# Spreading weight conversions over a loop, and moving preparation work by one step, in a clustered-attention and two-layer expert kernel

## The chip, the cores and the metric

The kernel runs on one core of a Trainium2 chip. A core has a matrix engine (TensorE, PE in the profile, with its weight loads as PEld), a vector engine (VectorE, DVE), an activation engine (ScalarE, ACT), a general engine (GpSimd, POOL) and a queue engine (SyncE, SP) that only starts transfers. Each engine takes its own instructions in the order in which the program gives them; engines wait for each other by semaphores. Transfers started by SP and by POOL are carried out by 16 DMA engines. The metric is the device time of one execution in microseconds; lower is better.

## What is computed

Three stages, one after the other, in float32:

```python
# 1. attention inside clusters: 2 batches x 8 heads, 768 positions, 64 wide, 16 centroids per head
q_assign = argmax(normalize(q) . normalize(centroids))     # k_assign likewise
scores = where(q_assign == k_assign, q @ k.T / 8, -1e9)
attn = softmax(scores) @ v                                 # -> x, 1536 tokens x 512
# 2. first layer: w_in 512 x 2048, w_out 2048 x 512
h = x @ w_in;  x = maximum(0.01 * h, h) @ w_out
# 3. mixture of 8 experts, top 1, with a skip test per token
skip = x @ w_skip;  e = argmax(x @ w_gate);  gate = softmax(x @ w_gate).max()
out = x + (skip > 0) * gate * (relu(x @ w1[e]) @ w2[e])
```

## The kernel before, in words

**Precision.** Most products are made in pieces. An operand is split into a rounded part (`hi`, in names `whii`, `whio`, `gh`, `xh`, `UA`) and the rest (`lo`, in names `wloi`, `wloo`, `gl`, `xl`), and three products are added: hi x hi, hi x lo, lo x hi. Splits are a copy on ACT (hi) and a subtraction on POOL or DVE (lo).

**Attention.** Eight pairs of heads (`p` = 0 to 7), each with 12 steps (`r` = 0 to 11, `s` = 12 p + r over all). A step takes 128 queries of one head against 768 keys. On PE it makes the scores (`st_scores`, L359: four matmuls from `UA`/`UB`, whose rows 64 to 79 hold the cluster mask, and from `VA`/`VB`, which hold the low parts), then the transposes of the probabilities of step s-3 (`st_transpose`, L414), and in every second step (r even) two pieces of attention x value for an earlier half pair (`st_av`, L433). DVE finds the row maximum, ACT makes the exponential (`st_exp`) and empties the transposes from PSUM (`st_evac`, tag T, two banks). For each half pair (`g`) the reciprocals of the row sums are transposed in `recip_rows` (L399; it too takes a bank of tag T), copied by ACT, written to a scratch in DRAM by SP, and read back spread over the partitions by POOL (`recip_load`), for `av_split` on POOL.

**Preparation of the next pairs** runs inside the steps of the pairs before. A table (`plan`, L311; `PREP`, `PREPS`) gives for each operation the step and one of four slots in a step (a0 and pa before the transposes, d and pb at the step's end). The operations are: transposes of raw q and k (`raw_pe`, PE, in bank M) and their copy (`raw_act`, ACT), the split (`raw_split`, POOL, followed by transfers on SP that rearrange halves, then `exchange`), cluster scores (`assign_pe`, `assign_act`), the argmax (`argmax_pe` on PE, `argmax_0` to `argmax_3` on DVE and POOL), the mask (`mask_pe`, `mask_dve`, `mask_dma`). `plan(d)` shifts all but the splits and exchanges by d steps. The tiles of tag M have one bank: who writes it next waits until the one before is read.

**Start.** Pair 0 is prepared ahead of the steps: its halves are exchanged by nine transfers inside the core (L490 to L504), six on SP and three on POOL, its cluster argmax runs on DVE, and `mask_first` (L272) writes the masks of queries (DVE) and keys (ACT) straight into `UA` and `UB`. Pair 1's raw copies and splits follow in the same stretch. An activation of one element (L505) loads the table of the exponential.

**Weights of the first layer.** `w_in` and `w_out` come as float64 words. 32 pieces (each 128 x 512) are loaded into staging buffers (`load_piece`, L534) and converted by five operations each (`convert_op`, L549): one on ACT (`cvu`, L557), four on DVE (L559, L561, L564, L570). Pieces 0 to 19 are converted during attention. The last twelve are converted in the first layer's loop by `conv_next(n)` (L671): it converts pairs of pieces until n of the twelve are done, and after each pair lets `load_next` put further loads on SP. Staging has two buffers for odd pieces (and, for the first, one even piece) and two for even ones; a load waits on SP until its buffer's last reader is done.

**First layer.** 48 iterations (3 blocks of 512 tokens x 16 chunks of the hidden width). Iteration i on PE: `m1_up(i)` (12 matmuls), then `m1_down(i-2)` (12 matmuls). On the others: `m1_act(i)` (`lk` on ACT, `g` on DVE, `gh` on ACT, `gl` on DVE), then the splits of the weights of i+2 (`split_i`, `split_o`: `whii` and `whio` on ACT, `wloi` and `wloo` on POOL), then `conv_next` by the line below. Chunk i=8 first reads pieces 1 to 4 of the twelve (split in iteration 6), i=12 the others (from iteration 10 on).

```python
conv_next(i + 3 if i % 2 else 0)      # before: i=1 converts four pieces, i=3, 5, 7, 9 two each
```

Of the kernel before, what the change touches and what calls it, by code (L numbers as in the profile page):

```python
# [15 lines left out]
ALU = mybir.AluOpType  # L16
AX = mybir.AxisListType
BIG = float(2.0 ** 60)
# [7 lines left out]
def kernel(  # L26
# [14 lines left out]
    nc = tc.nc  # L41
    B, H, S, D = q.shape
    NC_ = centroids.shape[1]
# [44 lines left out]
    HS = S // 2  # L88
# [82 lines left out]
    def raw_pe(p, i):  # L171
# [7 lines left out]
            nc.tensor.transpose(ps[:, j, :], src[:, 3 * half + j].rearrange("p h d -> p (h d)"), ident)  # L179
        ps_prep["raw", i] = ps  # L180

    def raw_act(p, i):
        qk, half = divmod(i, 2)
        ps = ps_prep.pop(("raw", i)).rearrange("p j c -> p (j c)")
        sc = SCALE if qk == 0 else 1.0
        nc.scalar.activation(out=raw_t[p][:, i, :], in_=ps, func=AF.Copy, scale=sc)
        if p == 1:
            raw_split(p, i)
            if half:
                exchange(p, qk)  # L190

    def first_hi(i):
        qk, half = divmod(i, 2)
# [6 lines left out]
    def raw_split(p, i):  # L200
        raw = raw_t[p]
        UA, UB, VA, VB = uv_t[p]
        qk, half = divmod(i, 2)
        cs = slice(half * HS, (half + 1) * HS)
        hi = UA[:, qk, cs]
        lo = (VA if qk == 0 else VB)[:, qk, cs]
        nc.gpsimd.tensor_scalar(out=hi, in0=raw[:, i, :], scalar1=1.0, scalar2=1.0, op0=ALU.mult, op1=ALU.mult)
        nc.gpsimd.tensor_tensor(out=lo, in0=raw[:, i, :], in1=_f(hi), op=ALU.subtract)
        if half == 1:
            dma = nc.sync.dma_start  # L210
            U, W, X, Y = (_f(t[:, qk, :]) for t in (UA, UB, VA, VB))
            dma(W[0:64], U[64:128])
            if qk == 0:
                dma(Y[0:64], X[64:128])
                dma(Y[64:128], U[64:128])
            else:
                dma(X[64:128], Y[0:64])
                dma(X[0:64], U[0:64])

    def exchange(p, qk):  # L220
        U, W, X, Y = (_f(t[:, qk, :]) for t in uv_t[p])
        if qk == 0:
            nc.sync.dma_start(X[64:128], U[0:64])
        else:
            nc.sync.dma_start(Y[0:64], W[0:64])
# [46 lines left out]
    def mask_first(h):  # L272
        U = uv_t[0][h]
        for qk in (1, 0):
            ps = (ps_m if h else ps_t)([P, S], "mps", BF16) if qk or not h else ps_a([P, S], "mps", BF16)
            for i in range(2):
                for j in range(3):
                    o = (3 * i + j) * P
                    nc.tensor.transpose(ps[64:64 + NC_, o:o + P], oh_t[0][:, j, 4 * qk + 2 * i + h, :], identb)
            ps = ps[64:64 + NC_, :]  # L280
            if qk:
                nc.scalar.activation(out=U[64:64 + NC_, 1, :], in_=ps, func=AF.Copy)
            else:
                nc.vector.tensor_scalar(out=U[64:64 + NC_, 0, :], in0=ps, scalar1=BIG, scalar2=-BIG,
                                        op0=ALU.mult, op1=ALU.add)

    def mask_pe(p):
        ps = ps_m([P, 3, P], "ohps", BF16)
# [22 lines left out]
    def plan(d):  # L311
        return [
            (d - 8, "pb", raw_pe, 0), (d - 7, "a0", raw_act, 0), (d - 7, "pb", raw_pe, 1),
            (d - 6, "a0", raw_act, 1), (d - 6, "pb", raw_pe, 2), (d - 5, "a0", raw_act, 2), (d - 5, "pb", raw_pe, 3),
            (d - 4, "a0", raw_act, 3), (d - 4, "pb", assign_pe, None),
            (d - 3, "a0", assign_act, None), (d - 3, "pb", argmax_pe, None),
            (d - 2, "d", argmax_0, None), (d - 2, "d", argmax_1, None), (d - 1, "d", argmax_2, None),
            (d, "d", argmax_3, None), (d + 1, "pb", mask_pe, None), (d + 2, "d", mask_dve, None),
            (0, "a0", raw_split, 0), (1, "a0", raw_split, 1), (2, "a0", raw_split, 2), (3, "a0", raw_split, 3),
            (3, "d", exchange, 0), (5, "d", exchange, 1), (max(d + 2, 5), "d", mask_dma, None),  # L320
        ]

    PREP = plan(0)
    PREP0 = [(3, "a0", assign_act, None), (3, "pb", argmax_pe, None), (4, "d", argmax_0, None), (4, "d", argmax_1, None),
             (5, "d", argmax_2, None), (6, "d", argmax_3, None)]
    PREP1 = [(1, "pb", assign_pe, None), (2, "a0", assign_act, None), (2, "pb", argmax_pe, None), (3, "pb", argmax_0, None), (4, "pb", argmax_1, None), (5, "d", argmax_2, None), (6, "pb", argmax_3, None), (7, "pb", mask_pe, None), (8, "d", mask_dve, None),
             (8, "d", mask_dma, None)]
    PREPS = {0: PREP0, 1: PREP1, 2: plan(4), 3: plan(2)}

    def prep(p, r, slot):  # L330
        if p >= NP:
            return
        for rr, sl, f, arg in PREPS.get(p, PREP):
            if rr == r and sl == slot:
                if arg is not None:
                    f(p, arg)
                else:
                    f(p)
                if f is raw_act and arg == 3 and 1 < p < NP - 1:
                    load_qk(p + 1)  # L340
# [141 lines left out]
    def first_lo(qk, halves=(0, 1)):  # L482
        for half in halves:
            cs = slice(half * HS, (half + 1) * HS)
            nc.vector.tensor_tensor(out=lo_k[:, half, :] if qk else VA[:, 0, cs], in0=raw_t[0][:, 2 * qk + half, :],
                                    in1=_f(UA[:, qk, cs]), op=ALU.subtract)

    Uq, Wq, Xq, Yq = (_f(t[:, 0, :]) for t in (UA, UB, VA, VB))
    Uk, Wk, Xk, Yk = (_f(t[:, 1, :]) for t in (UA, UB, VA, VB))
    nc.sync.dma_start(Wq[0:64], Uq[64:128])  # L490
    nc.sync.dma_start(Yq[64:128], Uq[64:128])
    first_lo(0, (0,))
    prep_cblk()
    first_lo(0, (1,))
    nc.sync.dma_start(Yq[0:64], Xq[64:128])
    nc.gpsimd.dma_start(Wk[0:64], Uk[64:128])
    nc.gpsimd.dma_start(Xk[0:64], Uk[0:64])
    nc.gpsimd.dma_start(Yk[0:64], Uk[64:128])
    assign_pe(0)
    first_lo(1)  # L500
    lo_kf = _f(lo_k.rearrange("p a b -> p (a b)"))
    nc.sync.dma_start(Xk[64:128], lo_kf[0:64])
    nc.sync.dma_start(Yk[64:128], lo_kf[64:128])
    nc.sync.dma_start(Xq[64:128], Uq[0:64])  # L504
    nc.scalar.activation(out=warm, in_=warm, func=AF.Exp)  # L505
    for r in range(3, 7):
        for slot in ("a0", "pa", "d", "pb"):
            prep(0, r, slot)
    load_v(0)
    for i in range(4):  # L510
# [2 lines left out]
    load_qk(2)  # L513
    mask_first(0)
    mask_first(1)

    chunks = {}
    ring_b = [None]
# [152 lines left out]
    def conv_next(n):  # L671
        while nxt[1] < min(n, len(pieces)):
            two = pieces[nxt[1]:nxt[1] + 2]
            for i_ in range(5):
                for pc in two:
                    convert_op(*pc, i_)
            nxt[1] += 2
            load_next(nxt[1] + (2 if wsp[0] is None else 4))

    for s in range(NSTEP + 12 + LAG):  # L680
        p, r = divmod(s, 12)
        if s < NSTEP:
            st_scores(s)
        conv_step(s, 0)
        preps(p, r, "a0")
        preps(p, r, "pa")
        if 0 <= s - LAG < NSTEP:
            st_transpose(s - LAG)
            st_evac(s - LAG)
        gf, rf = divmod(s, 6)  # L690
        if 0 < gf <= NSTEP // 6:
            if rf == 2:
                recip_rows(gf - 1)
            elif rf == 3:
                nc.sync.dma_start(rscr[gf - 1], rrow_t.pop(gf - 1))
        g, kt = divmod(s - 6 - LAG, 6)
        if 0 <= g < NSTEP // 6 and kt % 2:
            st_av(g, kt - 1)
            st_av(g, kt)
        if s < NSTEP:  # L700
            st_exp(s)
        if 0 <= g < NSTEP // 6 and kt == NT - 1:
            av_evac(g)
            av_split(g)
        if 0 <= g < NSTEP // 6 and kt == 3:
            recip_load(g)
        if 0 < gf <= NSTEP // 6 and rf < 2:
            recip(gf - 1, rf)
        preps(p, r, "d")
        preps(p, r, "pb")  # L710
        if r == 10 and p + 1 < NP:
            load_v(p + 1)
        conv_step(s, 1)
        if s == NSTEP:
            att_a.release()
            rt = pool("rt", "left")
            ring_b[0] = pool("ring_b", "left")
            wip[0] = pool("wi", "left")
            for c in range(NDIR // 4, NPC // 4):
                load_f32(c)  # L720
            load_next(2)
        if s == NSTEP + 4:
            for i in range(3):
                split_i(i)
# [301 lines left out]
    for i in range(NI):  # L1026
        if i == 14:
            r_consts()
        if i >= 2:
            m1_up(i)  # L1030
        for f, arg in sorted(r_tasks.get(i, ()), key=lambda x: x[1]):
            f(arg)
        step_gen(i, 0)
        if i >= 2:
            m1_down(i - 2)
        m1_act(i)
        step_gen(i, 1)
        if i + 2 < NI:
            if i:
                split_i(i + 2)  # L1040
            split_o(i + 2)
            g_, j_ = divmod(i + 2 - 2 * NFC, 4)
            if g_ >= 0 and j_ == 3:
                load_chunk(8 + 2 * g_)
                load_chunk(9 + 2 * g_)
        conv_next(i + 3 if i % 2 else 0)

    lb = NBLK - 1
    LT = lb * TPB
# [370 lines left out]
```

## Time and profile before

| | us |
|---|---|
| median of 3 runs (lowest to highest) | 690.68 (690.42 to 690.96) |
| the profiled execution | 689.63 |
| its span, first to last instruction | 687.9 |
| TensorE busy | 636.7 (93%) |
| ScalarE busy | 423.8 (62%) |
| VectorE busy | 407.4 (59%) |
| GpSimd busy | 278.2 (40%) |

Mean granted TensorE clock over the span: 0.985 of full speed. Attention's first scores start at 18.2 us, its last transposes end near 260, the first layer's loop runs from about 267 to about 555, the experts from there to the end. Times inside the span count from its start. Busy time of an engine is the sum of its instructions; PE's matmuls overlap and their ends are modelled. In a timeline a row shows start, duration, engine, line, operation, what it writes and reads, how often (rows of one kind that follow each other are merged), and in brackets the idle time of the engine before it and what ended that.

### The profile page before, as it was taken

What the parts mean: (1) busy time and instruction counts of PE and PEld (TensorE: products, weight loads), DVE (VectorE), ACT (ScalarE), POOL (GpSimd) and SP (SyncE); (2) the same over time, 40 slices, a digit from 0 to 9 for tenths busy, and PEclk for the clock granted to TensorE, in tenths of its full rate; (3) what the DMA queues carried; (4) which work ended last, traced back from release to release, by engine and by line L of the source; (5) the groups of instructions that cost most, each with busy time, mean ns of one, the idle gap of its engine ahead of it and who ended that gap; (6) DMA issues with size and microseconds to landing.
All of it is one profiled execution on the core that took longest, in us unless ns stands there. A gap on an engine that the chain in (4) does not pass through costs nothing. (4 is left out here: it accounts for less than half of the span.)

```text
span 687.9 us, 10140 instructions
## 1 busy us (share of the span) xinstructions
PE 636.7 (93%) x3587; PEld 491.8 (71%) x3587; DVE 407.4 (59%) x687; ACT 423.8 (62%) x824; POOL 278.2 (40%) x295
## 2 busy tenths in 40 slices
PE   5898999999999999499999999999999979989994
PEld 3676766666766666378888888788787868767873
DVE  5755858686776653767523213623226348999991
ACT  5887888897888885254445444445444436757870
POOL 4233636264553324363554444444444273002321
PEclk9999999999999999889999999999999999999997
DMA  8763764767656354221003000006303349989950
GB/s 196 184 189 95 196 163 140 187 172 193 167 153 171 111 183 144 104 111 61 1 3 122 1 1 0 1 0 245 122 3 122 123 163 362 339 280 333 357 192 25
DMA packets 62659, 98.31 MB, mean 143 GB/s; under 512 B 27593, under 2 KB 31659, under 8 KB 62224
## 3 DMA queue, kind: packets, MB, share of 16 engines
q1 hardware_dynamic: 59040, 88.13, 41.5%
q0 software_dynamic: 3568, 9.52, 4.2%
q8 instruction: 29, 0.48, 0.3%
q14 instruction: 22, 0.18, 0.1%
HBM read 72.47 MB, written 11.65 MB: 122 GB/s over the span
## 5 line engine op out<-in xcount | busy, mean ns | idle before, releaser
L369 DVE TENSOR_REDUCE st<-sps 128x1 f32<-128x768 f32 x96 | 91.5, 954 | 66.7 <-PE sps L366 66.3
L430 ACT ACTIVATE pt<-tps 128x384 f32<-128x384 f32 x192 | 84.8, 503 | 19.2 <-PE tps L423 18.6
L384 ACT ACTIVATE pr<-sps,st 128x768 f32<-128x768 f32 x96 | 87.7, 914 | 13.9 <-DVE st L369 13.4
L750 DVE TENSOR_TENSOR g<-ups,lk 128x512 f32<-128x512 f32 x48 | 33.1, 689 | 105.9 <-ACT lk L749 105.8
L634 POOL TENSOR_TENSOR wloi<-rawb,whii 128x512 fp32r<-128x512 f32 x36 | 46.7, 1298 | 115.4 <-ACT whii L632 115.4
L658 PE MATMUL ups<-xh,whii 128*128 128x512 f32 x192 | 76.0, 396 | 7.9 <-ACT whii L632 7.9
L423 PE MATMUL tps<-ident,pr 128*128 128x128 f32 x576 | 78.7, 273 | 0.5 <-ACT pt L430 0.5
L658 PE MATMUL ups<-xh,wloi 128*128 128x512 f32 x192 | 75.7, 394 | 1.4 <-POOL wloi L634 1.3
L658 PE MATMUL ups<-xl,whii 128*128 128x512 f32 x192 | 75.6, 394 | 0.0
L765 PE MATMUL acc<-whio,gh 128*128 128x512 f32 x184 | 73.4, 399 | 0.0
L765 PE MATMUL acc<-wloo,gh 128*128 128x512 f32 x184 | 71.8, 390 | 0.1
L423 PEld LDWEIGHTS tps<-ident,pr 128*128 128x128 f32 x576 | 68.4, 140 | 5.1 <-ACT pt L430 1.6
L438 PE MATMUL avps<-pt,vnat 128*64 128x384 f32 x384 | 71.9, 498 | 0.0
L765 PE MATMUL acc<-whio,gl 128*128 128x512 f32 x184 | 71.8, 390 | 0.0
L751 ACT ACTIVATE gh<-g 128x512 fp32r<-128x512 f32 x48 | 30.4, 632 | 51.9 <-DVE g L750 51.9
L749 ACT ACTIVATE lk<-ups 128x512 f32<-128x512 f32 x48 | 28.5, 593 | 50.9 <-PE ups L658 50.9
L752 DVE TENSOR_TENSOR gl<-g,gh 128x512 fp32r<-128x512 f32 x48 | 34.6, 721 | 33.5 <-ACT gh L751 33.5
L453 POOL TENSOR_TENSOR xr<-xr,rb 128x384 f32<-128x384 f32 x16 | 16.0, 1002 | 81.2 <-ACT xr L446 77.9
L658 PEld LDWEIGHTS ups<-xh,whii 128*128 128x128 f32 x192 | 36.6, 190 | 16.3 <-ACT whii L632 8.3
L644 POOL TENSOR_TENSOR wloo<-rawb,whio 128x512 fp32r<-128x512 f32 x36 | 47.0, 1304 | 0.8 <-ACT whio L643 0.8
L1171 POOL DMA_INDIRECT out_dram<-y,idx_s x8 | 13.6, 1695 | 76.8 <-DVE y L1169 36.0
L658 PEld LDWEIGHTS ups<-xh,wloi 128*128 128x128 f32 x192 | 36.6, 190 | 10.2 <-POOL wloi L634 2.6
(294 smaller groups left out, 1388.8 us busy)
## 6 DMA issues: line engine op xcount, KB each, us to landing
rawb<-in_moe_w_dram SPq DMA_DIRECT2D x26, 1024.0 KB, 6.9
stg<-in_moe_w_in_dram SPq DMA_DIRECT2D x16, 512.0 KB
stg<-in_moe_w_out_dram SPq DMA_DIRECT2D x16, 512.0 KB, 6.8
rawa<-in_moe_w_dram SPq DMA_DIRECT2D x8, 1024.0 KB
vnat<-in_v_dram SPq DMA_DIRECT2D x8, 384.0 KB, 3.7
rb<-recip_scratch POOLq DMA_DIRECT2D x32, 96.0 KB, 3.0
w_f_scratch<-cvt SPq DMA_DIRECT2D x12, 256.0 KB, 2.3
rawb<-w_f_scratch SPq DMA_DIRECT2D x3, 1024.0 KB
```

The costliest lines, as they stand in the source:

```text
L369: nc.vector.tensor_reduce(out=st[:, 0:1], in_=ps[:, :, 0:HS], axis=AX.XY, op=ALU.max, negate=True)
L384: nc.scalar.activation(out=pr, in_=ps[:, :, 0:HS], func=AF.Exp, bias=st[:, 0:1], accum_out=sm_t[g][:, 3 * h + j:3 * h + j + 1])
L423: nc.tensor.transpose(ps[:, t, :], pr[:, kh, t * P:(t + 1) * P], ident)
L430: nc.scalar.activation(out=pt[:, 3 * kh:3 * kh + 3, j, :], in_=t_t[s][kh], func=AF.Copy)
L438: nc.tensor.matmul(av_t[g][64 * h:64 * h + 64, :], lhsT=vnat[p][:, h, kt, :], rhs=pt_t[p, half, h][:, kt].rearrange("p j c -> p (j c)"), s ...
L634: eng.tensor_tensor(out=lo, in0=src, in1=_f(hi), op=ALU.subtract)
L644: nc.gpsimd.tensor_tensor(out=lo, in0=src, in1=_f(hi), op=ALU.subtract)
L658: nc.tensor.matmul(ps, lhsT=w[:, cc, :], rhs=x[:, cc, cs], start=(n == 0), stop=(n == 3 * KD - 1))
L750: nc.vector.tensor_tensor(out=g, in0=ps, in1=t, op=ALU.max)
L751: nc.scalar.activation(out=gh, in_=g, func=AF.Copy)
L752: nc.vector.tensor_tensor(out=gl, in0=g, in1=_f(gh), op=ALU.subtract)
L765: nc.tensor.matmul(ps, lhsT=a[:, ts_], rhs=w, start=(fc == 0 and n == 0), stop=(fc == NFC - 1 and n == 2))
```

## The change

Seven edits:

- `split_first` is new: pair 1's splits and exchanges are no longer issued inside `raw_act` but after `load_qk(2)` and `mask_first`. POOL's order stays; on SP the loads of pair 2 now come ahead of pair 1's transfers.
- `mask_first(0)` writes the query mask in two halves of 384 columns.
- `plan(0)`, `plan(4)`, `plan(2)` become `plan(1)`, `plan(5)`, `plan(3)`: one step later for pairs 4 to 7, 2 and 3.
- Two of the three POOL transfers of pair 0 go to SP, ahead of `first_lo`.
- The cluster copy `assign_act(0)` comes ahead of the activation that loads the exponential's table.
- `recip_rows` and the write of its row come one step later in each half pair (rf 3 and 4).
- `conv_next`: two pieces each at i = 1, 3, 5, 7, 8 and 9.

```diff
@@ -179,15 +179,16 @@
             nc.tensor.transpose(ps[:, j, :], src[:, 3 * half + j].rearrange("p h d -> p (h d)"), ident)
         ps_prep["raw", i] = ps
 
+    def split_first(p, i):
+        raw_split(p, i)
+        if i % 2:
+            exchange(p, i // 2)
+
     def raw_act(p, i):
         qk, half = divmod(i, 2)
         ps = ps_prep.pop(("raw", i)).rearrange("p j c -> p (j c)")
         sc = SCALE if qk == 0 else 1.0
         nc.scalar.activation(out=raw_t[p][:, i, :], in_=ps, func=AF.Copy, scale=sc)
-        if p == 1:
-            raw_split(p, i)
-            if half:
-                exchange(p, qk)
 
     def first_hi(i):
         qk, half = divmod(i, 2)
@@ -281,8 +282,9 @@
             if qk:
                 nc.scalar.activation(out=U[64:64 + NC_, 1, :], in_=ps, func=AF.Copy)
             else:
-                nc.vector.tensor_scalar(out=U[64:64 + NC_, 0, :], in0=ps, scalar1=BIG, scalar2=-BIG,
-                                        op0=ALU.mult, op1=ALU.add)
+                for cs in (slice(0, HS), slice(HS, S)) if h == 0 else (slice(0, S),):
+                    nc.vector.tensor_scalar(out=U[64:64 + NC_, 0, cs], in0=ps[:, cs], scalar1=BIG, scalar2=-BIG,
+                                            op0=ALU.mult, op1=ALU.add)
 
     def mask_pe(p):
         ps = ps_m([P, 3, P], "ohps", BF16)
@@ -320,12 +322,12 @@
             (3, "d", exchange, 0), (5, "d", exchange, 1), (max(d + 2, 5), "d", mask_dma, None),
         ]
 
-    PREP = plan(0)
+    PREP = plan(1)
     PREP0 = [(3, "a0", assign_act, None), (3, "pb", argmax_pe, None), (4, "d", argmax_0, None), (4, "d", argmax_1, None),
              (5, "d", argmax_2, None), (6, "d", argmax_3, None)]
     PREP1 = [(1, "pb", assign_pe, None), (2, "a0", assign_act, None), (2, "pb", argmax_pe, None), (3, "pb", argmax_0, None), (4, "pb", argmax_1, None), (5, "d", argmax_2, None), (6, "pb", argmax_3, None), (7, "pb", mask_pe, None), (8, "d", mask_dve, None),
              (8, "d", mask_dma, None)]
-    PREPS = {0: PREP0, 1: PREP1, 2: plan(4), 3: plan(2)}
+    PREPS = {0: PREP0, 1: PREP1, 2: plan(5), 3: plan(3)}
 
     def prep(p, r, slot):
         if p >= NP:
@@ -489,22 +491,24 @@
     Uk, Wk, Xk, Yk = (_f(t[:, 1, :]) for t in (UA, UB, VA, VB))
     nc.sync.dma_start(Wq[0:64], Uq[64:128])
     nc.sync.dma_start(Yq[64:128], Uq[64:128])
+    nc.sync.dma_start(Wk[0:64], Uk[64:128])
+    nc.sync.dma_start(Yk[0:64], Uk[64:128])
     first_lo(0, (0,))
     prep_cblk()
     first_lo(0, (1,))
     nc.sync.dma_start(Yq[0:64], Xq[64:128])
-    nc.gpsimd.dma_start(Wk[0:64], Uk[64:128])
     nc.gpsimd.dma_start(Xk[0:64], Uk[0:64])
-    nc.gpsimd.dma_start(Yk[0:64], Uk[64:128])
     assign_pe(0)
     first_lo(1)
     lo_kf = _f(lo_k.rearrange("p a b -> p (a b)"))
     nc.sync.dma_start(Xk[64:128], lo_kf[0:64])
     nc.sync.dma_start(Yk[64:128], lo_kf[64:128])
     nc.sync.dma_start(Xq[64:128], Uq[0:64])
+    prep(0, 3, "a0")
     nc.scalar.activation(out=warm, in_=warm, func=AF.Exp)
-    for r in range(3, 7):
-        for slot in ("a0", "pa", "d", "pb"):
+    prep(0, 3, "pb")
+    for r in range(4, 7):
+        for slot in ("d", "pb"):
             prep(0, r, slot)
     load_v(0)
     for i in range(4):
@@ -513,6 +517,8 @@
     load_qk(2)
     mask_first(0)
     mask_first(1)
+    for i in range(4):
+        split_first(1, i)
 
     chunks = {}
     ring_b = [None]
@@ -689,9 +695,9 @@
             st_evac(s - LAG)
         gf, rf = divmod(s, 6)
         if 0 < gf <= NSTEP // 6:
-            if rf == 2:
+            if rf == 3:
                 recip_rows(gf - 1)
-            elif rf == 3:
+            elif rf == 4:
                 nc.sync.dma_start(rscr[gf - 1], rrow_t.pop(gf - 1))
         g, kt = divmod(s - 6 - LAG, 6)
         if 0 <= g < NSTEP // 6 and kt % 2:
@@ -1043,7 +1049,7 @@
             if g_ >= 0 and j_ == 3:
                 load_chunk(8 + 2 * g_)
                 load_chunk(9 + 2 * g_)
-        conv_next(i + 3 if i % 2 else 0)
+        conv_next({1: 2, 3: 4, 5: 6, 7: 8, 8: 10, 9: 12}.get(i, 0))
 
     lb = NBLK - 1
     LT = lb * TPB
```

## Rows read from the trace of the kernel before

**Rows 1.** The page: busy tenths of PE in 40 equal slices.
```profile
PE   5898999999999999499999999999999979989994
```
**Rows 2.** Stretches: length, busy by engine (instructions), granted clock, DMA share, GB/s.
```profile
106.04:136.97 30.93, 29.41 (x200) 21.20 (x197) 22.24 (x34) 26.31 (x61) 14.90 (x19) 1.00 0.60 160
...
266.49:285.18 18.69, 17.25 (x74) 13.29 (x72) 12.85 (x14) 7.35 (x13) 11.34 (x11) 1.00 0.16 49
285.18:293.08 7.90, 0.00 (x0) 0.00 (x1) 4.64 (x9) 2.35 (x5) 0.00 (x0) 0.68 0.62 227
293.08:298.40 5.32, 5.19 (x12) 3.67 (x13) 2.87 (x5) 3.75 (x7) 4.90 (x4) 0.51 0.30 119
...
342.90:348.34 5.44, 5.44 (x26) 4.50 (x25) 1.38 (x2) 2.39 (x5) 2.54 (x2) 1.00 0.00 0
```
**Rows 3.** Waits from 266 to 300: us in total, times, longest.
```profile
PE ups L658 <- ACT whii L632: 7.9, 1, 7.9
...
PE ups L658 <- POOL wloi L634: 1.3, 1, 1.3
```
**Rows 4.** Timeline around the gap, engines SP, DVE and ACT.
```profile
266.59 17.17 SPq L544 DMA_DIRECT2D stg<-in_moe_w_out_dram  x2
...
276.00 2.72 DVE L559 TENSOR_SCALAR cvu<-cvu 128x512 f32<-128x512 f32 x2
...
283.89 0.41 DVE L559 TENSOR_SCALAR cvu<-cvu 128x512 f32<-128x512 f32 x1
...
287.05 0.66 ACT L557 ACTIVATE cvu<-stg 128x512 f32<-128x512 f32 x1 [6.22 <-DMA stg<-in_moe_w_out_dram]
...
292.42 0.61 ACT L632 ACTIVATE whii<-rawb 128x512 fp32r<-128x512 f32 x1
```
**Rows 5.** Timeline of one conversion in the steady loop, ACT, DVE and POOL.
```profile
307.49 1.20 ACT L557 ACTIVATE cvu<-stg 128x512 f32<-128x512 f32 x2
...
308.17 1.91 DVE L559 TENSOR_SCALAR cvu<-cvu 128x512 f32<-128x512 f32 x2 [1.11 <-ACT cvu L557]
...
309.73 0.60 ACT L749 ACTIVATE lk<-ups 128x512 f32<-128x512 f32 x1 [1.04 <-PE ups L658]
...
313.08 0.68 DVE L750 TENSOR_TENSOR g<-ups,lk 128x512 f32<-128x512 f32 x1
...
314.33 0.62 ACT L632 ACTIVATE whii<-rawb 128x512 fp32r<-128x512 f32 x1
...
315.03 1.29 POOL L634 TENSOR_TENSOR wloi<-rawb,whii 128x512 fp32r<-128x512 f32 x1 [5.56 <-ACT whii L632]
```
**Rows 6.** Waits during attention, 18 to 254.5: us in total, times, longest.
```profile
PE rcps L401 <- ACT pt L430: 10.8, 15, 1.1
```
**Rows 7.** Timeline of PE and ACT around `recip_rows`, a steady pair.
```profile
143.59 0.33 PE L401 MATMUL rcps<-ident,rc 128*128 128x128 f32 x1 [0.39 <-ACT pt L430]
...
146.61 0.87 ACT L430 ACTIVATE pt<-tps 128x384 f32<-128x384 f32 x2 [0.41 <-PE tps L423]
...
159.34 0.33 PE L401 MATMUL rcps<-ident,rc 128*128 128x128 f32 x1 [1.13 <-ACT pt L430]
```
**Rows 8.** Timeline of PE, ACT and DVE in pairs 1 and 2.
```profile
55.83 0.90 ACT L384 ACTIVATE pr<-sps,st 128x768 f32<-128x768 f32 x1 [1.22 <-DVE st L369]
...
60.07 0.67 DVE L296 TENSOR_SCALAR mk<-ohps,msc 128x384 fp32r<-128x384 bf16 x1
...
60.84 0.52 PE L179 MATMUL rawps<-ident,natq 128*128 128x128 f32 x3 [0.90 <-issue]
...
88.75 0.96 DVE L369 TENSOR_REDUCE st<-sps 128x1 f32<-128x768 f32 x1 [1.32 <-PE sps L366]
```
**Rows 9.** Timeline of SP, ACT and PE at the start.
```profile
13.05 0.70 SPq L504 DMA_DIRECT2D VA<-UA  x1
...
17.24 0.80 ACT L282 ACTIVATE UA<-mps 16x768 fp32r<-16x768 bf16 x1 [1.61 <-DMA VB<-UA]
...
19.05 0.59 PE L366 MATMUL sps<-VA 128*128 128x384 f32 x2 [0.23 <-DMA VA<-UA]
```

## The prediction

> **What bounds the kernel now.** I read the page's slices first: TensorE (PE) is at nine tenths or more in most of the 40 slices, with two places to look at, the start and slice 16 (the first is slice 0), a 4 in the middle of a row of nines [rows 1]. Then the busy times by stretch: in the middle of attention PE is busy 29.41 of 30.93 us, and an iteration of the first expert layer's loop is 5.44 of 5.44 [rows 2]. So PE sets the time nearly everywhere, and a change pays only where PE stands still. From 285.18 to 293.08 it does nothing for 7.90 us, and in the 5.32 us after that its granted clock is 0.51, the lower of the two levels (1.2 GHz): twelve matmuls take 5.32 us where half an iteration, 2.72 us, is the price at the upper level [rows 2]. The list of waits names the gap: PE waits 7.9 us, once, for ScalarE's (ACT) `whii` [rows 3].
>
> The timeline says why [rows 4]. In iteration i=1 `conv_next` converts four staged pieces. The sync queue (SP) can load the fourth only when the first is converted and its buffer free: its two issues end at 283.76. ACT, which works in order, stands 6.22 us before that piece's first operation (287.05), and behind that operation wait `lk` of i=2, `gh` and `whii` (292.42), for which PE waits. Nothing before iteration 6 reads what pieces three and four become.
>
> **The change part by part.** Sums are made against the profiled execution: its span is 687.9, its time 689.63, so 1.73 lies around the span; the median of the runs is 690.68, 1.05 above it.
>
> *Conversions spread: the gap.* With two pieces at i=1, ACT goes from the second piece's operation straight to `lk`. VectorE (DVE) ends the first two pieces at 283.89 [rows 4], and `g` starts there. `whii` follows 1.25 us after the start of `g` (313.08 to 314.33) and takes 0.62; GpSimd's (POOL) `wloi` follows another 0.70 later and takes 1.29 [rows 5]. So whii starts at 285.15 and is done at 285.8, wloi at 287.1. PE comes free at 285.18, does two matmuls from 285.8 and stands for the third until 287.1: 1.5 us lost in place of the 7.9. With gaps of that size the clock should stay up: before 285.18 PE also waited 1.3 us, for a wloi, and the granted clock of that stretch is 1.00 [rows 2, 3]. Before, the stretch from 285.18 to 298.40 was 13.22 us for 2.72 us of work, 10.5 lost; now 1.5. Gain 9.0. Bounds: 10.5 if whii comes in time, and 6.4 if the clock falls all the same (2.6 of the 9.0).
>
> *The moved conversions.* Pieces three and four now convert at i=3, where before five and six did. No work is added there, but DVE starts them about 2.0 us later against PE than in the steady loop, because `g` and `gl` of i=2 and 3 are late. The slack there is some 1.8 us: wloi is done at 316.3; PE ended a product at 309.6 (just before `lk`, 309.73) and comes to the third matmul that reads this wloi 0.4 after three half iterations, at 318.1 [rows 5]. I charge 0.2. At i=7, 8 and 9 three conversions follow each other. One takes DVE from 308.17 to 313.08, 4.9 us [rows 5]. The first is covered as now. With a second right behind it, ACT's two operations start when `whio` is done, at 315.4, DVE 0.68 after them (as at 307.49 and 308.17) at 316.05, until 320.95; whii is done at 322.8 and wloi at 324.2. PE would want that at 323.5 (309.6, five half iterations, 0.4): 0.7 lost. So each further conversion ends 7.9 us after the one before, against 5.44 for an iteration: the third ends at 328.8, its wloi at 332.1, and without any stall PE would be there at 328.9. Lost in all 3.2. Bounds: 0, if the lag is covered, and 12.2, if a conversion takes 7.9 us itself, as the first one did (276.00 to 283.89 [rows 4]): each of the three then adds 3.0. I take 3.2, from the nearer row, the steady loop. Behind the waiting `g` on DVE are `gl` and the next conversion; `gh` and `whii` wait for `g`, and PE for those.
>
> The Trainium skill bears on this in SBUF — State Buffer (section SBUF: two separate sides): VectorE and GpSimd share a pair of ports, and whichever starts first keeps it for its whole instruction. The trace agrees in direction: two of the same DVE operation take 2.72 us at 276.00 and 1.91 at 308.17, where one takes 0.41 at 283.89.
>
> *`recip_rows` and the preparation one step later.* `recip_rows` needs a bank of tag T that ACT has just to empty; PE waits for it 10.8 us in 15 of its 16 calls [rows 6]. In the step r=2 that wait is 0.39, in r=8 it is 1.13, because ACT has a conversion's operation and a `raw_act` before it empties the bank [rows 7]. In r=3 ACT starts emptying at 146.61 and has the first bank free after half of 0.87 us, while PE has been ready since about 146.66: 0.4, no gain against r=2. In r=9 no conversion's operation lies before, but a raw_act still does; I put it between the two, at 0.6. Eight calls at 0.4 and seven at 0.6 make 7.4 of the 10.8: 3.4 gained. Bounds: 0 and 6.
>
> `raw_pe(0)` shares bank M with the mask's transposes and waits until DVE has read them. Pair 0 loses that wait, since pair 1's plan stays and pair 2's moves from step 8 to 9: about 0.6 gained. In pair 1 PE waited 0.9 us for the mask (done at 60.74, PE at 60.84), behind attention-value matmuls; in the new step 7 none of them cover DVE's reduction and mask, and the wait is about 1.4, 0.5 lost. Against that, `argmax_2` no longer holds DVE up a step early (ACT waited 1.22 us for the maximum behind it): 1.2 gained. In pair 2 the mask was covered in step 4; in step 5 it isn't: the reduction (88.75) starts about 1.0 after the step's scores and lasts 0.87 to the next operation, then come `cvt` with 0.4 and the mask with 0.67 [rows 8], 3.0 in all against PE ready some 1.4 after the scores: 1.5 lost. Together 0.2 lost; between 2 lost and 2 gained. `mask_dma`, `load_qk` and the write of the reciprocals move too. Each is issued at least two steps before its reader; on SP the write now stands behind `exchange`, half a microsecond of issue. At the end of attention POOL reads the last reciprocals only after `av_split` of the half before, so a later write stays hidden; if it doesn't, one step is 1.5.
>
> *The start.* The key mask on ACT waited 1.61 us, until 17.24, for a transfer of the POOL queue. With that gone, the query mask in halves and the cluster copy ahead of the table load, the first scores could run up to 1.6 earlier. But their second product waits at 19.05 for a transfer into `VA`, issued on SP at 13.05 [rows 9], and that one waits for an earlier SP transfer, ahead of which two new issues of 0.6 us are put. So the wait changes its name: from 1.6 gained to 1.2 lost; I take 0, since the last landing stays SP's. `load_qk(2)` now goes ahead of pair 1's transfers, which are needed twelve steps later. `split_first` changes nothing in POOL's own order.
>
> Sum: 9.0 - 0.2 - 3.2 + 3.4 - 0.2 + 0 = 8.8. Span 679.1, execution 680.8, median of runs 681.9.
>
> **The rivals.**
> *The row of conversions costs nothing.* For it: POOL's work moves along with the chain. Against: 7.9 us of chain in 5.44. 3.2 less, and with attention's upper bound 2.6 less again: 676.1 to 678.7.
> *The clock falls all the same, or ACT meets a late piece at i=3.* 2.6 for the clock and 1 to 1.5 of waiting: 685.7. Against it: pieces three and four landed by 287.05, and i=3 asks for them after that.
> *POOL holds each conversion twice.* Without the 1.1 us that POOL costs the operations at 308.17 a conversion is 3.8; two subtractions of 1.3, waited for in full, make it 6.4, so 1.5 three times, 4.5 more: 686.4. Against it: the steady conversions lie beside POOL already, at 4.9. (This is what the lock in the Trainium skill's SBUF — State Buffer would do at its worst.)
> *Slower.* Place: iterations 8 to 11. If each of the three conversions takes 7.9 us, the loss there is 12.2, and PE stands long enough in one piece for the low clock, 2.6 more: 14.8 against 9.0 - 0.2 + 3.2 = 12.0: 693.5. It decides from 7.0 us per conversion on (3.2 + 3 x 2.1 + 2.6 = 12.1).
> *The change doesn't do what it says:* the gap stays, since `g` of i=2 is late anyway, and the rest cancels: 689.5 to 691.9.
>
> **How the numbers follow.** The forecast 0.50, its own range 679.5 to 684.5; faster than that 0.13; the clock or a late piece 0.16; POOL's holds 0.07; no change 0.06; slower 0.08. What lies within 0.2%, 1.4 us, a measurement of this kernel can't tell from no change. So faster 0.86, same 0.06, slower 0.08. The range goes from 677.0, the middle of the first rival, to 687.5, past POOL's holds, and leaves out under 2 in 10.
>
> **What would show it.** Slice 16 full, no wait of PE for `whii` above 2 us there and no clock of 0.5; then new waits of PE for whii and wloi, together about 3 us, in iterations 9 to 11. PE's waits at `recip_rows` down to some 7 us, steps r=3 and r=9 longer and r=8 shorter. A new wait of PE for `mk` in pair 2's step 5. The first scores' second product within 1 us of 19.05. I am wrong if the gap is closed and attention is longer than before, or if the three conversions open a gap of their own.

## The result, and the profile after

| | before | after |
|---|---|---|
| median of 3 runs (lowest to highest) | 690.68 (690.42 to 690.96) | 682.86 (682.46 to 683.77) |
| the profiled execution / its span | 689.63 / 687.9 | 682.86 / 681.2 |
| mean granted clock | 0.985 | 0.988 |

Ratio 0.9889, 95% interval 0.9867 to 0.9912: faster, by 1.1%. The forecast was 681.9 in 677.0 to 687.5, with a span of 679.1; the span came out 2.1 longer.

The page after, PE and its clock in 40 slices, against [rows 1]:

```profile
PE   5999999999999999899899999999999979989994
PEclk9999999999999999999999999999999979999998
```

The 4 of slice 16 is an 8, but three slices further, where there was a 9, is another 8. Stretches after, with the columns of [rows 2]: a steady pair; the old gap (two rows); then the three iterations between the starts of up-projections 10, 11, 12 and 13.

```profile
105.71:136.18 30.47, 29.43 (x199) 21.02 (x198) 22.06 (x34) 25.70 (x61) 16.07 (x19) 1.00 0.58 147
...
281.15:284.51 3.36, 2.13 (x8) 1.16 (x7) 1.39 (x2) 2.60 (x6) 2.33 (x2) 1.00 0.95 377
284.51:288.65 4.14, 4.14 (x20) 3.38 (x18) 3.24 (x5) 2.63 (x5) 2.95 (x3) 1.00 0.15 62
315.90:322.84 6.94, 5.63 (x26) 4.25 (x24) 6.21 (x10) 2.24 (x5) 1.74 (x2) 1.00 0.08 32
322.84:330.77 7.93, 6.01 (x24) 4.34 (x24) 6.31 (x11) 3.26 (x7) 2.71 (x2) 1.00 0.01 2
330.77:337.24 6.47, 5.85 (x24) 4.54 (x25) 2.70 (x5) 4.33 (x8) 5.08 (x4) 1.00 0.00 0
```

The gap is shut and the clock stays at its upper level there. But three iterations that should take 5.44 each take 6.94, 7.93 and 6.47: 5.02 lost. Waits of PE after: attention (18 to 250.5), the old gap (262 to 300), the row (300 to 340).

```profile
PE rcps L403 <- ACT pt L432: 7.0, 15, 1.0
...
PE ups L664 <- POOL wloi L640: 1.9, 2, 1.3
PE ups L664 <- ACT whii L638: 0.6, 1, 0.6
...
PE ups L664 <- ACT whii L638: 2.6, 2, 1.3
PE ups L664 <- POOL wloi L640: 1.2, 2, 0.6
```

The 7.9 of [rows 3] is 0.6 now (whii) plus 0.6 (wloi; the 1.3 is the one that stood there before). The 2.6 and 1.2 in the row are new. Each stop costs some 0.3 more than its wait: matmuls just behind one are spaced wider (0.35 at 282.15, where 0.23 is usual).

The table has all runs below; each number but the time is a difference of first-matmul starts in the profiled execution. *Attention* is pair 0's and the later pairs' time, from the first scores to up-projection 0; *gap* is up-projections 3 to 6 less 3 x 5.44; *row* is 10 to 13 less 3 x 5.44; *rest* is from 13 to the end of the span. Time is the median of that kernel's runs (short_first: one).

| kernel | attention | gap | row | rest | time |
|---|---|---|---|---|---|
| before | 248.3 | 12.44 | 0.00 | 343.1 | 690.7 |
| after | 244.5 | 3.42 | 5.02 | 343.9 | 682.9 |
| after_again | 245.2 | 3.40 | 6.69 | 345.7 | 683.7 |
| conv_alone | 248.2 | 3.39 | 5.03 | 343.2 | 688.1 |
| conv_undone | 245.1 | 13.05 | 0.00 | 342.9 | 686.0 |
| recip_undone | 249.0 | 3.43 | 6.65 | 344.7 | 689.4 |
| start_undone | 245.7 | 3.41 | 5.03 | 344.9 | 684.5 |
| short_first | 245.2 | 3.73 | 3.43 | 346.9 | 684.6 |
| conv_even | 247.1 | 3.41 | 0.07 | 343.0 | 677.7 |
| even_again | 245.2 | 3.40 | 0.05 | 344.4 | 678.0 |
| even_plan4 | 244.7 | 3.40 | 0.09 | 343.2 | 678.4 |
| even_plan42 | 244.0 | 3.41 | 0.07 | 342.9 | 676.7 |
| even_oldprep | 242.5 | 3.41 | 0.06 | 344.5 | 676.3 |

From before to after: attention 3.8, gap 9.0, row -5.0, rest -0.8, together 7.0; the first scores start 0.2 later, and the span fell by 6.8. (In conv_even's attention 2 us are a low clock in pair 0's first steps.)

### The profile page after: what moved, and what is told of

The parts are those of the page before. It is cut to its first block, busy times and chain, and to the rows that moved or that the text cites. A ratio compares the mean times of both kernels' runs of the same rounds, so it can differ in the third digit from the quotient of the medians.

```text
span 681.2 us, 10131 instructions
## 1 busy us (share of the span) xinstructions
PE 638.6 (94%) x3587; PEld 491.6 (72%) x3587; DVE 407.5 (60%) x688; ACT 420.1 (62%) x824; POOL 282.5 (41%) x293
## 5 line engine op out<-in xcount | busy, mean ns | idle before, releaser
L757 ACT ACTIVATE gh<-g 128x512 fp32r<-128x512 f32 x48 | 30.3, 632 | 64.8 <-DVE g L756 64.8
L984 DVE TENSOR_TENSOR xl<-rawb,xh 128x1024 fp32r<-128x1024 f32 x36 | 42.3, 1215 | 0.3 <-ACT xh L982 0.3
```

Of the source, the lines that this page charges most:

```text
L984: eng.tensor_tensor(out=lo, in0=src, in1=_f(hi), op=ALU.subtract)
```

## The experiments

**conv_alone and conv_undone: do the parts add up?** One is the kernel before with the new list of conversions, the other the kernel after with the old one:

```diff
-        conv_next(i + 3 if i % 2 else 0)
+        conv_next({1: 2, 3: 4, 5: 6, 7: 8, 8: 10, 9: 12}.get(i, 0))
```

> The kernel before with the new list of conversions and nothing else. Theory (the parts add up): the gap at i=2..4 is worth 9.1 us, the row of conversions at i=7, 8, 9 costs 5.0, so 4.1 less than before, 686.6 us; PE's waits at recip_rows stay at 10.8. Rival (the row costs the 3.2 that was forecast, and the other 1.8 of loss seen after came with other parts): 684.8. Rival (the attention part's gain is needed to make the gap close): 688 or more.

> The changed kernel with the old list of conversions. Theory (the parts add up): it keeps attention's 3.6 us and nothing else, so the gap of 7.9 us for whii and the stretch of low clock are back, and there is no loss at i=8 to 11: 687.0 us, 4.1 slower than the changed kernel. Rival (the changed start and preparation are worth something past attention too): under 686. Rival (attention's gain is lost again at the gap, because the pieces land at the same time as before): 690.

688.14 (ratio to before 0.9968, 0.9954 to 0.9981) and 685.96 (0.9943, 0.9926 to 0.9959). The table has the parts where they were expected: gap 3.39 and row 5.03 in the one, 13.05 and 0.00 in the other, whatever attention does. conv_undone came out 1.0 under the 687.0 expected, at the edge of its rival's 686. By the profiles that is *rest*, 342.9 where the kernel after has 343.9, with code that no edit touches, so the parts don't bear the rival out. conv_undone has its old wait, of the kernel's waits in 262 to 305 the first:

```profile
PE ups L664 <- ACT whii L638: 8.1, 1, 8.1
```

conv_alone's median is 1.5 above the sum of 686.6; its profiled execution was the fastest of ten (685.55), so that part can't be shown.

**conv_even: is the loss that of the row?** Kernel after with

```diff
-        conv_next({1: 2, 3: 4, 5: 6, 7: 8, 8: 10, 9: 12}.get(i, 0))
+        conv_next(i + 1 if i % 2 and i < 12 else 0)
```

> The changed kernel with its six conversions at i=1, 3, 5, 7, 9, 11, so no two in a row. Theory (the loss of 5.0 us between up-projections 10 and 13 is the row's): it is gone, up-projections keep 5.44 us apart up to iteration 13, 677.9 us. Rival (the row itself costs 3.2, the other 1.8 is a loop that runs late anyway): 679.7. Rival (a conversion at i=11 meets the first rows of the next chunk or the router's work and opens a gap of its own): 681 or more.

> The changed kernel with conversions at i=1, 3, 5, 7, 9, 11 once more, on the chip of the next two: 677.7 us, with no more than 0.1 us lost before any of up-projections 10 to 14, whatever the clock does elsewhere.

677.70 and, on another chip, 678.01 (ratios to before 0.9819, 0.98 to 0.9837, and 0.9806, 0.979 to 0.9823). conv_even's stretches between up-projections 10 and 13:

```profile
317.08:322.57 5.49, 5.49 (x25) 4.43 (x24) 3.94 (x6) 3.28 (x6) 4.34 (x4) 1.00 0.12 43
322.57:328.01 5.44, 5.44 (x25) 4.50 (x24) 3.91 (x8) 2.16 (x4) 0.99 (x1) 1.00 0.00 0
328.01:333.48 5.47, 5.47 (x26) 4.43 (x24) 3.93 (x6) 3.27 (x6) 4.33 (x4) 1.00 0.00 0
```

PE is full. The row cost 5.0, not 3.2, and no other gap opens at i=11.

**short_first: where do the other 1.8 come from?** In the kernel before, the conversion at i=5, that of [rows 5], starts on DVE 1.42 after the first matmul of up-projection 6, the first row here; in the kernel after it starts 2.94 after it, and that of i=7 2.93 after up-projection 8's. Timeline of the kernel before, PE:

```profile
306.75 0.39 PE L658 MATMUL ups<-xh,whii 128*128 128x512 f32 x1
```

Timeline of the kernel after, PE, ACT and DVE, from the first conversion into the row:

```profile
272.38 2.68 DVE L565 TENSOR_SCALAR cvu<-cvu 128x512 f32<-128x512 f32 x2 [0.20 <-ACT cvu L563]
...
280.24 0.68 DVE L756 TENSOR_TENSOR g<-ups,lk 128x512 f32<-128x512 f32 x1
...
286.13 2.00 DVE L565 TENSOR_SCALAR cvu<-cvu 128x512 f32<-128x512 f32 x2 [0.88 <-ACT cvu L563]
...
294.09 0.39 PE L664 MATMUL ups<-xh,whii 128*128 128x512 f32 x1
...
297.03 2.01 DVE L565 TENSOR_SCALAR cvu<-cvu 128x512 f32<-128x512 f32 x2 [0.86 <-ACT cvu L563]
...
297.46 0.58 ACT L755 ACTIVATE lk<-ups 128x512 f32<-128x512 f32 x1
...
302.04 0.68 DVE L756 TENSOR_TENSOR g<-ups,lk 128x512 f32<-128x512 f32 x1
...
314.20 0.62 ACT L638 ACTIVATE whii<-rawb 128x512 fp32r<-128x512 f32 x1
...
322.17 0.61 ACT L638 ACTIVATE whii<-rawb 128x512 fp32r<-128x512 f32 x1
...
330.11 0.61 ACT L638 ACTIVATE whii<-rawb 128x512 fp32r<-128x512 f32 x1
```

`lk` at 297.46 has no idle time ahead of it, where that of [rows 5] had waited 1.04 for PE: ACT is behind. From one conversion to the next (286.13, 297.03) pass 10.90, and PE wants 10.88 for two iterations: the lateness that i=1 leaves is not made up. In between neither ACT nor DVE waits for PE, only each for the other. Lateness alone costs nothing: in conv_even the conversion at i=9 still starts 2.97 after its up-projection (320.05, 317.08), and PE is full. The experiment takes it away: the first pair of pieces keeps ACT's operation and the last of DVE's only (which then reads `cvu`).

```diff
-            for i_ in range(5):
+            for i_ in (range(5) if nxt[1] else (0, 4)):
```

> The changed kernel with VectorE's first three operations left out for the first two pieces, at i=1 (their values are then wrong; nothing else changes): that conversion is some 5 us shorter on VectorE. Theory (the loop carries its lateness: a conversion and the two iterations around it are a chain of 10.9 us, as long as the 10.88 that PE needs for them, so nothing is made up): the 1.2 us lost at up-projection 4 are gone, the conversion at i=5 starts within 1.6 us of the start of its up-projection on PE, not 2.9, and the row at i=7, 8, 9 costs 3.2 to 3.6 us in place of 5.0; 680 us. Rival (the loop makes lateness up by i=7): the row costs 5.0 all the same; 681.6.

The row: 3.43, where the forecast's steady loop said 3.2. Its timeline has ACT's slack back, and DVE starts 1.42 after PE, as before; its stretches (the gap's first iteration, then the row's three) show what is left of the stops:

```profile
294.47 0.39 PE L665 MATMUL ups<-xh,whii 128*128 128x512 f32 x1
...
295.89 1.89 DVE L565 TENSOR_SCALAR cvu<-cvu 128x512 f32<-128x512 f32 x2 [0.98 <-ACT cvu L563]
...
297.45 0.60 ACT L756 ACTIVATE lk<-ups 128x512 f32<-128x512 f32 x1 [1.02 <-PE ups L665]
```

```profile
274.42:283.59 9.17, 7.34 (x25) 5.56 (x24) 4.64 (x5) 3.40 (x6) 6.55 (x5) 0.81 0.49 172
...
316.23:321.67 5.44, 5.44 (x25) 4.43 (x24) 4.74 (x9) 1.32 (x3) 0.21 (x2) 1.00 0.00 0
321.67:329.51 7.84, 5.92 (x26) 4.25 (x25) 6.22 (x11) 3.16 (x7) 2.64 (x2) 1.00 0.01 2
329.51:335.98 6.47, 5.85 (x24) 4.53 (x25) 2.69 (x5) 4.32 (x8) 5.08 (x4) 1.00 0.00 0
```

The expected time of 680 was missed (684.57, a single run): PE's wait for whii at up-projection 4 is gone, but the clock was at 0.81 in the first of these stretches, behind a wait for wloi of 1.8 us (1.3 in the kernel after), and *rest* is 3.0 longer than after, again with a low clock (below). Up-projection 4 thus started 1.4 later than after (283.59, 282.15), so a part of DVE's lateness went because PE was late, and not by the shorter conversion. What the run shows, in one execution, is the price of the row without lateness; the time shows nothing.

**recip_undone: recip_rows or the preparation?** Kernel after with

```diff
-            if rf == 3:
+            if rf == 2:
                 recip_rows(gf - 1)
-            elif rf == 4:
+            elif rf == 3:
```

> The changed kernel with recip_rows and its write back at steps 2 and 3 of six. Theory (the gain in attention is recip_rows'): PE's waits there go from 7.0 us back to 10.8 and attention is 3.6 longer, 686.5 us. Rival (the wait shrank because the preparation was moved away from ACT's step 8): at most 1 us longer, 683.9. Rival (the shifted preparation and the old recip_rows meet in one step): more than 5 us longer, 688.

689.41 (ratio to before 0.9984, 0.9972 to 0.9997). The wait in attention is nearly back to the 10.8 of [rows 6]:

```profile
PE rcps L403 <- ACT pt L432: 10.5, 15, 1.1
```

Attention is 4.5 longer than after, where 3.6 was expected, and 0.7 longer than before: moving the preparation alone loses. The time, 6.6 longer, passes the last rival's 5, but attention doesn't: by the profiles 1.6 of it is the row, 6.65 here, with a low clock as in the next run, and 0.8 is *rest*.

**after_again and start_undone.** The kernel after once more, and with the start undone (Wk and Yk back on POOL's queue, the table load ahead of the cluster copy, the query mask whole):

```diff
-    nc.sync.dma_start(Wk[0:64], Uk[64:128])
-    nc.sync.dma_start(Yk[0:64], Uk[64:128])
...
+    nc.gpsimd.dma_start(Wk[0:64], Uk[64:128])
     nc.gpsimd.dma_start(Xk[0:64], Uk[0:64])
+    nc.gpsimd.dma_start(Yk[0:64], Uk[64:128])
...
-    prep(0, 3, "a0")
     nc.scalar.activation(out=warm, in_=warm, func=AF.Exp)
```

> The changed kernel once more, on the chip of the next three. Theory (the low-clock stretches after short stalls come and go between executions of one program): the losses before up-projections 11, 12 and 13 are again 5.0 us by start to start, but the clock's stretches in the profile lie elsewhere than in the first profile, and the median of more runs lies within 1 us of 682.9. Rival (the clock follows the program alone): the same stretches, 19.6 us at the start and 10.2 us at the experts' first matmuls.

> The changed kernel with its four start edits undone (two transfers back on POOL's queue, the table load before the cluster copy, the query mask whole), the preparation's shift kept. Theory (the wait changes its name only): pair 1's first scores within 0.4 us of the changed kernel's at the same rise of the clock, 683.0 us. Rival (the edits gain up to 1 us, which the first profile of the changed kernel hid under a late rise of the clock): 683.8. Rival (they lose what two issues cost on SP): 682.0.

683.70 (681.71 to 685.96) and 684.49 (682.95 to 686.74): not told apart. Pair 1's first scores come at 40.41 and 41.13; with the new start and the new preparation they lie at 40.00 to 40.76 in six profiles, at 41.83 where the clock was low in pair 0's first steps, and with the old start at 40.81 to 41.13 in three. But two of these three (before and conv_alone) have the older preparation and `recip_rows` too, which make pair 0's steps from the third on 0.5 longer (19.20 in place of 18.68). The third step's scores, ahead of that, start at 21.32 to 22.47 in the ten profiles with the new start and at 21.61 to 22.44 in the three with the old: no gain of the start is shown. Another 0.9 of start_undone's attention is one step of the last pair, where ACT waits 1.18 for a weight piece (228.55). `split_first` stays in this run, and no run undoes it alone.

after_again has the row's loss of after, and 1.6 more, in its last iteration, at a lower clock; in start_undone (two rows below) the low clock lies one iteration earlier:

```profile
315.53:322.49 6.96, 5.70 (x25) 4.24 (x23) 6.19 (x10) 2.27 (x6) 1.76 (x2) 1.00 0.09 34
322.49:330.44 7.95, 6.02 (x25) 4.35 (x25) 6.32 (x11) 3.28 (x7) 2.73 (x2) 1.00 0.01 2
330.44:338.53 8.09, 7.47 (x24) 5.73 (x25) 2.73 (x5) 4.35 (x8) 5.05 (x4) 0.79 0.00 0
```

```profile
324.34:332.43 8.09, 7.46 (x24) 5.65 (x25) 6.47 (x11) 3.43 (x7) 2.83 (x3) 0.79 0.01 2
332.43:338.76 6.33, 5.76 (x25) 4.43 (x25) 2.54 (x4) 4.17 (x8) 4.95 (x4) 1.00 0.00 0
```

So one program has its last stretch at 1.00 in one execution and at 0.79 in another: the row sometimes costs 6.7. One iteration earlier the same low clock costs nothing (row 5.03 in start_undone, and in conv_alone, which has it there too): PE would have waited in that iteration anyway. Of what was expected of after_again, the loss of 5.0 was missed, and the rival is half right: the experts' start, 216 to 228 us behind up-projection 13, has a granted clock of 0.61 here and 0.62 in the first profile.

**even_plan4, even_plan42 and even_oldprep: the preparation.** conv_even with older plans:

```diff
-    PREPS = {0: PREP0, 1: PREP1, 2: plan(5), 3: plan(3)}
+    PREPS = {0: PREP0, 1: PREP1, 2: plan(4), 3: plan(3)}     # even_plan4
+    PREPS = {0: PREP0, 1: PREP1, 2: plan(4), 3: plan(2)}     # even_plan42 and even_oldprep
-    PREP = plan(1)
+    PREP = plan(0)                                           # even_oldprep
```

> No two conversions in a row, and pair 2's preparation back to the older plan, one step earlier, so that its mask is again made in step 4, beside attention-value matmuls. Theory (the mask in step 5 has no cover): pair 2 takes 31.2 us in place of 32.58, with no wait of PE for mk; 676.4 us. Rival (its raw transposes or its reduction now meet recip_rows in step 3 or 9): pair 2 no shorter than 32.4, 677.7. Rival (pair 1 is made longer by the earlier plan as much as pair 2 is shorter): pair 1 above 33.5, 677.7.

678.40, no change: a miss of mine. Key 2 acts while pairs 0 and 1 run; it made pair 1 1.0 shorter (31.43) and pair 0 1.2 longer (23.41; 1.1 by its steps from the third on), and left pair 2 at 32.60. The wait that I meant hangs on key 3.

> No two conversions in a row, and both special plans back to the older ones (the plan of the key 3 acts during pair 2, that of key 2 during pair 1: the run before put back only key 2). Theory (the mask made in pair 2's step 5 has no cover): pair 2 takes 31.2 us in place of 32.6 and PE's wait for mk in step 5 is gone; pair 0 stays 1.2 longer and pair 1 1.0 shorter, as in the run before; 676.4 us. Rival (recip_rows in step 3 meets the mask in step 4, and takes the gain back): pair 2 no shorter than 32.2, 677.7.

676.74, pair 2 31.08 (32.58 after): the theory's 31.2. The mask's missing cover costs 1.5, but pair 1 was 32.49 again (its step 6 takes 4.24, where it took 3.00 in even_plan4), so attention in all gains 1.2 on even_again.

> No two conversions in a row, recip_rows one step later, and the preparation of every pair back where it was. Theory (the two moves add up; the shift of the preparation alone makes attention 0.7 us longer, as the steps of the kernel with recip_rows put back show): a pair in the middle of attention takes 30.3 us (30.47 with both moves, 30.93 with neither, 31.08 with the preparation alone), 676.6 us in all. Rival (recip_rows gains only if the raw evacuation of step 8 goes to step 9, out of its way): 30.9 or more per pair, and 680 us.

676.33 (ratio to before 0.9786, 0.977 to 0.9803; lowest to highest 675.83 to 676.83), the lowest median here, some 7 us below after (even_plan42's executions, 676.16 to 678.98, overlap its own). A steady pair takes 30.0 us, under the 30.3 expected. Its wait in attention and one steady pair:

```profile
PE rcps L403 <- ACT pt L432: 5.6, 15, 1.2
```

```profile
135.60:165.66 30.06, 29.36 (x200) 21.06 (x198) 22.41 (x34) 26.00 (x61) 15.20 (x19) 1.00 0.68 180
```

## Why the prediction was right, and where not

*The time.* It came out 1.0 above the forecast, the span 2.1. The difference is luck: the forecast carried over the 1.05 by which the median of before lay above its profiled execution, and in the kernel after the profiled execution is the median.

*The gap: right.* 12.44 lost before, 3.42 after: 9.0, where the forecast had 9.0 less 0.2. The two waits that it worked out at up-projection 4, 0.6 for whii and by its times 0.8 for wloi, are in the list at 0.6 each, and the conversion at i=3 opened nothing beyond them. conv_undone brings the loss back.

*Conversions in a row: the mis-sized term.* 3.2 forecast, 5.0 measured (conv_even takes all of it away). The spacing was right: whii at 314.20, 322.17 and 330.11, so 7.97 and 7.94 per further conversion where 7.9 stood. The step that failed is the first: "The first is covered as now." I took the steady loop's state of before, where a conversion starts 1.42 after PE; in the kernel after it starts 2.94 after. The forecast itself had DVE 2.0 late at i=3, set that against a slack of 1.8 and charged 0.2, and then let the lateness go. It doesn't go: one conversion and two iterations of `lk`, `g`, `gh`, `whii`, `whio` are 10.90 end to end. In short_first, without lateness, the first conversion in the row is covered and the row is 3.43.

*recip_rows and the preparation: the sum right, the parts not.* Forecast 3.4 and -0.2, so 3.2; measured 3.8 of attention. The wait fell to 7.0, where 7.4 was forecast, but not as forecast: in a steady pair r=3 stands 0.72 (0.4 forecast), r=9 0.31 (0.6). The 0.4 holds with the older preparation (0.38 to 0.44 in even_oldprep's steady pairs); the rest of the 0.72 came with the shift. And the parts depend on their order: with the new preparation recip_rows is worth 4.5 (recip_undone), with the old one 5.8 (248.3 to 242.5); the shift of the preparation costs 0.7 without recip_rows' move and 2.0 with it. Counted from the third step's scores on, which leaves out the low clock of the first steps, these four are 4.3, 6.0, 0.5 and 2.2. So recip_rows was worth at least 0.9 more than forecast, the shift cost at least 0.3 more, and they partly cancelled: that the sum came out is luck. Where the forecast looked, at pairs 0 to 2, it had the shift alone nearly right: by recip_undone 0.8 and 0.8 gained and 1.6 lost, where 0.6, 0.7 and 1.5 stood. It put the steady pairs at nothing, and these lose 0.15 each by the shift alone (31.08, 30.93 before) and 0.4 to 0.5 each beside the moved recip_rows (30.47, against 29.99 to 30.06 in even_oldprep). The new wait for the mask in pair 2 is there as worked out, 1.4 against 1.5. Timeline of PE and DVE in pair 2 and of the two steps of `recip_rows`, after, against [rows 7, 8]:

```profile
88.45 0.42 DVE L567 TENSOR_SCALAR cvt<-cvu 128x512 uint32<-128x512 uint32 x1
88.78 0.67 DVE L298 TENSOR_SCALAR mk<-ohps,msc 128x384 fp32r<-128x384 bf16 x1
...
89.55 0.52 PE L179 MATMUL rawps<-ident,natq 128*128 128x128 f32 x3 [1.36 <-issue]
...
145.99 0.33 PE L403 MATMUL rcps<-ident,rc 128*128 128x128 f32 x1 [0.72 <-ACT pt L432]
...
160.95 0.33 PE L403 MATMUL rcps<-ident,rc 128*128 128x128 f32 x1 [0.31 <-ACT pt L432]
```

*The start: right within its bounds.* The second product runs 0.18 later than in [rows 9], the key mask no longer waits for a transfer, and no run shows the start to be worth anything either way. Timeline after:

```profile
15.76 2.73 PE L280 MATMUL mps<-identb,oh 128*16 128x128 bf16 x24 [1.14 <-DVE oh L269]
15.96 0.46 SPq L506 DMA_DIRECT2D VA<-UA  x1
...
16.61 0.80 ACT L283 ACTIVATE UA<-mps 16x768 fp32r<-16x768 bf16 x1 [1.45 <-PE mps L280]
...
19.23 0.67 PE L368 MATMUL sps<-VA 128*128 128x384 f32 x2
```

*The rivals.* That the row costs nothing fell, and so did that of no change. POOL's holds fell too: by the spacing a conversion in the row takes 7.97 with everything around it, as forecast, and DVE's part is 307.93 to 312.95, 315.92 to 320.93 and 323.89 to 328.86, 5.0 each, not 6.4. The Trainium skill's SBUF — State Buffer (section SBUF: two separate sides) states an exclusive lock on the pair of ports that VectorE and GpSimd share, held for a whole instruction. This trace agrees in direction, most of all where POOL works without a break: the first conversion, beside POOL's work from 270.34 to 277.6, takes 7.86 again, and its first two pairs of operations 2.68 and 2.92, where the next conversion's take 2.00 and 0.75. The slower rival's conditions came half true: DVE's 5.0 didn't become 7.9, but a stretch of low clock behind the row is real in some executions, 1.6 us of the 2.6 that was feared.

*Rest.* 0.8 was lost behind the row with no change to that code. The same 12 us of the experts' start (216 to 228 us behind up-projection 13), before, after and in short_first, by the granted clock:

```profile
560.83:572.83 12.00, 10.05 (x56) 8.61 (x57) 7.02 (x26) 2.64 (x6) 8.79 (x9) 0.86 0.64 233
```

```profile
553.24:565.24 12.00, 10.45 (x51) 9.13 (x52) 6.16 (x22) 1.52 (x4) 8.75 (x9) 0.62 0.65 233
```

```profile
551.98:563.98 12.00, 8.73 (x36) 7.73 (x37) 5.47 (x18) 1.01 (x3) 8.76 (x9) 0.50 0.57 199
```

*Rest* goes with it in these three: 343.1, 343.9 and 346.9. The clock isn't all of it: after_again has 0.61 there and 345.7, and 1.0 of its 1.8 over the first profile is a longer wait of PE for `exi`, of its waits in 570 to 600 the first; it is 0.2 in that profile:

```profile
PE yps L1168 <- DVE exi L1197: 1.2, 1, 1.2
```

Nor is it tied to the row: even_again has no row and 344.4. What decides it from one execution to the next stays open.

## What to carry to other kernels

A chain of in-order engines that is exactly as long as the bound's period (10.90 us against 10.88 here) hides its work but makes nothing up: a delay met once is carried to the next place where slack is wanted, so take a term's starting state from the kernel after the edits before it, not from the steady loop of the kernel before. When work is spread, space it evenly at the period at which it is known to be hidden; three in a row gave back 5.0 of the 9.0 won. And test edits of one stage apart as well as together: here one edit's gain hid another's loss of 2.

## What the runs showed of the hardware that was not expected

One program gets its clock in different places from one execution to the next: behind the row 1.00 in one profile of the kernel after and 0.79 in the other, with the same waits ahead of it. In thirteen profiles the time from up-projection 13 to the end lay between 342.9 and 346.9 us with that code unchanged. Executions of one kernel spread over as much as 4.3 us (681.71 to 685.96 for the kernel after), so that terms under 1 us were to be read from the traces' own stretches and not from the times.
